# Fixed program order on four engines, with the products interleaved by hand, in a Fourier-mixing and dense-block kernel

## The chip, the cores and the metric

The kernel runs on one core of a Trainium2 chip. The metric is the time of one execution on the device in microseconds (us); lower is better. "Stop" below means time in which TensorE starts no matmul although its program has more of them. The profile calls TensorE PE, VectorE DVE, ScalarE ACT and GpSimd POOL.

## The reference, cut to what matters

```python
X = np.fft.rfft(x, axis=1)                    # x: (8, 3008, 256)
Y = X * (filt_r + 1j * filt_i)[None, :, :]
y = np.fft.irfft(Y, n=3008, axis=1)
h = y.reshape(24064, 256) @ w_in              # (256, 2048)
g = h - np.tanh(h)
return g @ w_out                              # (2048, 256)
```

## The kernel before

All arithmetic is in float32. The Fourier transforms are matmuls: `first` and `middle` (matmuls named pf, pz, pe) and `last` (pu). The two dense layers use a seven-product scheme for 2 x 2 blocks. The dense part is cut into 48 groups of tokens and 4 steps per group, 192 steps in all. In one **slot** of the loop the kernel does `up` of step U, the activation `shrink` of step U-1 and `down` of step U-2, and it weaves in the transform of the next batch unit. All transform matmuls share one PSUM bank, `up` has the three banks x, y and z, `down` the other four. X1 below is product 1 of `up`, into bank x, Y2 product 2, into bank y, and so on; p1 and p5 are ScalarE's copies of products 1 and 5 of `down`. Here is the code, shortened:

```python
    def up(U, between):
        ...
        mm(X, 1, True)
        s1 = copied("s1")             # ScalarE: PSUM -> SBUF
        mm(Y, 2, True)
        between(0)
        V.tensor_add(h[:, 0, :, 0:w], Y, s1)
        mm(X, 6, False)               # adds onto X; may start when s1 is copied
        between(1)
        u2 = copied("u2")
        mm(Z, 5, True)
        between(2)
        mm(X, 7, False)
        u3 = copied("u3")
        between(3)
        V.tensor_add(h[:, 3, :, 0:w], Z, u3)
        mm(X, 4, False)
        between(4)
        V.tensor_copy(h[:, 2, :, 0:w], X)
        mm(Z, 3, False)
        V.tensor_add(h[:, 1, :, 0:w], Z, u2)

    def shrink(U):
        for k in (2, 0):              # the two halves of h
            ACT.activation(y[k], ht[k], AF.Arctan, scale=S)
            ACT.activation(y[k], y[k], AF.Square)
            yield
            V.tensor_mul(ht[k], ht[k], y[k])
            ACT.activation(sq[k], y[k], AF.Square, bias=near_b, scale=A)
            yield
            V.scalar_tensor_tensor(out=ht[k], in0=sq[k], scalar=K, in1=ht[k], ...)
        combine(blocks, ...)          # GpSimd: four subtractions
        yield

    def down(U):                      # done: the last of a group's four steps
        mm(1, 2)
        if done: ACT.copy(p1, product(1)); V.tensor_add(...)
        yield
        mm(3, 5)
        if done: ACT.copy(p5, product(5)); V.tensor_add(...)
        yield
        mm(6, 7)
        if done: V.tensor_add(...) x2; G.tensor_add(...) x2
        yield
        mm(4)
        if done: V.tensor_add(...); store(i, o)     # two transposes on VectorE, then DMAs
        yield
```

`between(k)` takes one step of `down`, one of `shrink` and those transform steps that are due. The code only states what depends on what: a scheduler at compile time decides the order on each engine. I call the slot in which `down` finishes a group, one in four, the **closing slot**.

## Time and profile before

| | |
|---|---|
| median of 3 runs | 3037.85 us (3034.25 to 3043.77) |
| TensorE busy, of a span of 3035.6 us | 2789.7 us |
| dense part, first to last matmul | 211 to 3013 us |
| of it lost to stops and slow clock | 183 us |

From the start of each TensorE record to the start of the next I subtract the stream time of its shape (0.216 us for 256 columns). What remains is first put down to the halved clock where the trace grants one (0.50 of the full clock in its records); what then is under 0.15 us counts as "small"; the rest goes to the wait that ended it. Before: 72 us z on VectorE, 53 small, 17 slow clock, 16 x on VectorE's copy, 11 x on ScalarE's u copies, 7 transform matmuls, 6 others; with roundings 183. (The prediction took fixed ends, 210 and 3000 us, and found 180.)

How ScalarE got through a closing slot is in the timeline (start, duration, then what ran):

```profile
424.80 0.59 ACT L456 COPY u<-x 128x512 f32<-128x512 f32 x1
425.28 0.38 ACT L543 COPY p<-o 128x256 f32<-128x256 f32 x1
425.54 1.16 ACT L494 ACTIVATE sq<-y,near_b 128x1024 f32<-128x1024 f32 x1
```

The scheduler put the u copy, which TensorE needs, ahead of p5 and sq.

### The profile page before, as it was taken

The numbers are of one execution on the slowest core, as the hardware profiler recorded it, in microseconds if no ns is written. First come the engines' busy times: TensorE is split into PE (matmuls) and PEld (weight loads), VectorE is DVE, ScalarE is ACT, GpSimd is POOL, SyncE is SP. The second block draws the span as 40 slices with busy tenths as digits, with TensorE's granted clock in tenths as the row PEclk, the third lists the DMA queues.
The fourth block names the chain that finished last, engine by engine and source line by source line (L and its number), as shares of the span: only waits on it lengthen the run. The fifth ranks groups of instructions, "written<-read, shape, count | busy, mean of one in ns | idle before, by whom it ended". The sixth has DMA issues, their size and how long they took to land.

```text
span 3035.6 us, 36258 instructions
## 1 busy us (share of the span) xinstructions
PE 2789.7 (92%) x12410; PEld 2261.0 (74%) x12410; DVE 1845.8 (61%) x2382; ACT 1822.8 (60%) x2432; POOL 1602.4 (53%) x1398
## 2 busy tenths in 40 slices
PE   2369999999999999999999999999999999999996
PEld 0247766887877777887877777788888878888886
DVE  4865565665655555665665565666666666666664
ACT  1336666666666666666666666656666666666563
POOL 4653676534465566554455565645455555544543
PEclk6569999999999999999999999999999999999998
DMA  9744343222222322222322222222122212110100
GB/s 165 268 119 131 98 117 109 80 75 80 74 69 57 76 78 60 65 61 83 86 58 61 69 74 61 69 60 61 44 50 57 73 46 51 32 27 14 21 8 15
DMA packets 328867, 220.32 MB, mean 73 GB/s; under 512 B 228305, under 2 KB 282581, under 8 KB 328322
## 3 DMA queue, kind: packets, MB, share of 16 engines
q1 hardware_dynamic: 272848, 151.84, 20.1%
q10 hardware_dynamic: 53202, 50.35, 5.5%
q0 software_dynamic: 2624, 15.73, 2.0%
q8 instruction: 100, 1.64, 0.2%
q14 instruction: 93, 0.76, 0.1%
HBM read 134.41 MB, written 83.36 MB: 72 GB/s over the span
## 4 chain that ended last, share of the span: by engine, by line
PE 76%; POOL 6%; ACT 5%; DVE 5%; DMA 4%; issue 3%; ACTq 0%; SPq 0%; POOLq 0%; DVEq 0%
PE o L526 32%; PE x L450 19%; PE z L450 9%; PE y L450 5%; PE pe L338 3%; PE pu L414 3%; PE pz L357 3%; POOL t L429 2%; PE pf L283 2%; DVE h L496 1%; POOL uv L374 1%; DMA ct<-a 1%; ACT sq L494 1%; DMA w<-in_moe_w_in_dram 1%; POOL o L550 1%
## 5 line engine op out<-in xcount | busy, mean ns | idle before, releaser
L526 PE MATMUL o<-t,wd 128*128 128x256 f32 (+2 forms) x3072 | 777.4, 375 | 0.5 <-POOL t L430 0.5
L429 POOL TENSOR_TENSOR t<-h 128x512 f32<-128x512 f32 (+2 forms) x192 | 239.3, 1246 | 847.0 <-DVE h L496 754.2
L526 PEld LDWEIGHTS o<-t,wd 128*128 128x128 f32 x3072 | 577.7, 190 | 77.9 <-issue 7.8
L490 ACT ACTIVATE y<-h 128x1024 f32<-128x1024 f32 (+2 forms) x384 | 385.1, 1032 | 384.4 <-DVE h L475 384.1
L450 PE MATMUL x<-tu,wu 128*128 128x256 f32 (+2 forms) x2304 | 593.8, 378 | 6.2 <-ACT u L456 6.0
L526 PE MATMUL o<-h,wd 128*128 128x256 f32 (+2 forms) x2304 | 585.5, 376 | 3.0 <-DVE h L496 2.9
L496 DVE SCALAR_TENSOR_TENSOR h<-sq,h 128x1024 f32<-128x1024 f32 (+2 forms) x384 | 474.7, 1236 | 181.5 <-ACT sq L494 175.5
L450 PEld LDWEIGHTS x<-tu,wu 128*128 128x128 f32 x2304 | 424.2, 190 | 157.2 <-issue 84.1
L493 DVE TENSOR_TENSOR h<-h,y 128x1024 f32<-128x1024 f32 (+2 forms) x384 | 469.3, 1247 | 66.4 <-ACT y L491 64.1
L526 PEld LDWEIGHTS o<-h,wd 128*128 128x128 f32 x2304 | 436.5, 191 | 60.0 <-DVE h L496 5.3
L494 ACT ACTIVATE sq<-y,near_b 128x1024 f32<-128x1024 f32 (+2 forms) x384 | 433.8, 1130 | 76.1 <-DVE h L496 71.6
L491 ACT ACTIVATE y<-y 128x1024 f32<-128x1024 f32 (+2 forms) x384 | 386.2, 1036 | 0.9
L456 ACT COPY u<-x 128x512 f32<-128x512 f32 (+2 forms) x384 | 219.7, 572 | 217.1 <-PE x L450 206.8
L463 DVE TENSOR_TENSOR h<-y,s 128x512 f32<-128x512 f32 (+2 forms) x192 | 130.3, 679 | 268.2 <-ACT s L456 206.2
L373 POOL TENSOR_TENSOR zs<-zs,ft 128x512 f32<-128x512 f32 x112 | 143.5, 1282 | 249.1 <-ACT zs L371 234.3
L450 PE MATMUL z<-ut,wu 128*128 128x256 f32 (+2 forms) x768 | 200.5, 382 | 65.2 <-DVE h L472 64.9
L432 POOL TENSOR_TENSOR t<-t,h 128x512 f32<-128x512 f32 (+2 forms) x192 | 245.3, 1278 | 10.4
L472 DVE TENSOR_TENSOR h<-z,u 128x512 f32<-128x512 f32 (+2 forms) x192 | 129.4, 674 | 194.9 <-ACT u L456 194.9
L430 POOL TENSOR_TENSOR t<-h,t 128x512 f32<-128x512 f32 (+2 forms) x192 | 239.7, 1249 | 0.0
L431 POOL TENSOR_TENSOR t<-h 128x512 f32<-128x512 f32 (+2 forms) x192 | 239.6, 1248 | 0.0
L450 PE MATMUL x<-ut,wu 128*128 128x256 f32 (+2 forms) x768 | 218.1, 408 | 11.1 <-DVE h L475 10.7
L450 PEld LDWEIGHTS z<-ut,wu 128*128 128x128 f32 x768 | 140.5, 190 | 100.8 <-DVE h L472 82.9
(96 smaller groups left out, 3360.5 us busy)
## 6 DMA issues: line engine op xcount, KB each, us to landing
a<-ct SPq DMA_DIRECT2D x64, 384.0 KB, 3.8
ct<-e ACTq DMA_DIRECT2D x128, 192.0 KB, 2.2
ft<-filt SPq DMA_DIRECT2D x48, 512.0 KB, 4.2
out_dram<-ot SPq DMA_DIRECT2D x1408, 16.0 KB, 1.5
x_sb<-in_x_dram SPq DMA_DIRECT2D x69, 256.0 KB, 2.8
ct<-a ACTq DMA_DIRECT2D x69, 256.0 KB, 2.7
e<-ct SPq DMA_DIRECT2D x33, 512.0 KB, 4.1
filt<-filt_sb POOLq DMA_DIRECT2D x2, 4096.0 KB, 16.1
```

The source lines that it names most:

```text
L429: G.tensor_sub(t[0], b[0][1], b[0][0])
L430: G.tensor_sub(t[1], b[1][1], t[0])
L431: G.tensor_sub(t[2], b[1][1], b[0][1])
L432: G.tensor_sub(t[3], t[1], b[1][0])
L450: nc.tensor.matmul(bank[:, k], wu[:, q - 1, (2 * u + k) * 128:(2 * u + k + 1) * 128], rhs[q - 1], start=(first and k == 0), stop=True, ski ...
L456: ACT.copy(t, X)
L490: ACT.activation(y[k], ht[k], AF.Arctan, scale=S)
L491: ACT.activation(y[k], y[k], AF.Square)
L493: V.tensor_mul(ht[k], ht[k], y[k])
L494: ACT.activation(sq[k], y[k], AF.Square, bias=near_b, scale=A)
L496: V.scalar_tensor_tensor(out=ht[k], in0=sq[k], scalar=K, in1=ht[k], op0=ALU.add, op1=ALU.mult)
L526: nc.tensor.matmul(product(q), wd[:, q - 1, (2 * u + k) * 128: (2 * u + k + 1) * 128], rhs[q - 1][:, k], start=(u == 0 and k == 0 and q == ...
```

## The change

Its intent: take the order on TensorE, ScalarE, VectorE and GpSimd from the program text, and write that text so that a product and the one that depends on it are far apart. It has three parts: **(S)** strict order, **(I)** a new interleave, **(D)** the store of a group deferred to the next slot.

```diff
+            order = {nc.tensor.engine, ACT.engine, V.engine, G.engine}
+            with tc.manual_schedule(engines=order):                     # S
 ...
         mm(Y, 2, True)
-        between(0)
+        d()                                                             # I: one step of down
+        s()                                                             #    one step of shrink
         V.tensor_add(h[:, 0, :, 0:w], Y, s1)
+        t(0)                                                            #    transform steps due
         mm(X, 6, False)
-        between(1)
+        mm(Z, 5, True)
+        d()
+        s()
         u2 = copied("u2")
-        mm(Z, 5, True)
-        between(2)
+        t(1)
         mm(X, 7, False)
+        s()
         u3 = copied("u3")
-        between(3)
         V.tensor_add(h[:, 3, :, 0:w], Z, u3)
+        s()
+        d()
+        t(2)
         mm(X, 4, False)
-        between(4)
         V.tensor_copy(h[:, 2, :, 0:w], X)
+        s()
+        d()
+        t(3)
         mm(Z, 3, False)
 ...
-            store(i, o)
+            stores.append((i, o))                                       # D
 ...
+                        if k == 1 and stores:
+                            store(*stores.pop())
```

`shrink` is cut at other places too (the end of the first half goes with the start of the second). The places of `last` and of a range test at the end shift a little with the new gaps. I call the place of `t(k)` **gap k**.

More of the change, by code (lines that the diff above doesn't have):

```diff
@@ L435, with up @@
     hs, gs = {}, {}
-    def up(U, between):
+    def up(U, d, s, t):
         i, u = divmod(U, 4)
@@ L487, in shrink, with start, square, end @@
         y, sq = {}, {}
-        for k in (2, 0):
-            y[k], sq[k] = tiles("y", 2), tiles("sq", 1)
+        def start(k):
+            y[k] = tiles("y", 2)
             ACT.activation(y[k], ht[k], AF.Arctan, scale=S)
             ACT.activation(y[k], y[k], AF.Square)
-            yield
+        def square(k):
+            sq[k] = tiles("sq", 1)
             V.tensor_mul(ht[k], ht[k], y[k])
             ACT.activation(sq[k], y[k], AF.Square, bias=near_b, scale=A)
-            yield
+        def end(k):
             V.scalar_tensor_tensor(out=ht[k], in0=sq[k], scalar=K, in1=ht[k],
                                    op0=ALU.add, op1=ALU.mult)
+        start(2)
+        yield
+        square(2)
+        yield
+        end(2)
+        start(0)
+        yield
+        square(0)
+        yield
+        end(0)
         t = dn.tile([128, 4, 2, 256], F32, tag="t", bufs=2, name="t")
@@ L502, in shrink @@
         yield
-    accs = {}
+    accs, stores = {}, []
     def down(U):
@@ L754 @@
             total = 4 * len(groups)
-            for U in range(total + 2):
-                i, u = divmod(U, 4)
-                if U < total:
-                    p, c = groups[i]
-                    if c == 0 and u == 0:
-                        units = 4 * len(CHUNKS[p])
-                        steps, done = [], 0
-                        if p + 1 < len(UNITS):
-                            n_f = len(chunks_of(UNITS[p + 1], XH))
-                            n_m = 2 * NK // (3 - len(UNITS[p + 1]))
-                            steps = [(0.02 + 0.26 * k / n_f) * 4 * units for k in range(n_f)]
-                            lo, hi = 0.34 * 4 * units, 4 * units - 14
-                            steps += [lo + (hi - lo) * k / n_m for k in range(n_m)]
-                            fs, ms = first(p + 1, z1), None
-                    if u == 0 and i + 1 < len(groups) and c + 1 < len(CHUNKS[p]):
-                        e2s[i + 1] = load_e2(*groups[i + 1])
-                    if u == 2 and i + 1 < len(groups) and c + 1 == len(CHUNKS[p]):
-                        e2s[i + 1] = load_e2(*groups[i + 1])
-                    if u == 2 and i + 1 < len(groups):
-                        lasts = last(i + 1, z1)
-                sh = shrink(U - 1) if 0 <= U - 1 < total else iter(())
-                dw = down(U - 2) if 0 <= U - 2 < total else iter(())
-                def between(k):
-                    nonlocal ms, done
-                    if k < 4:
-                        next(dw, None)
-                    next(sh, None)
-                    if U >= total:
-                        return
-                    if k < 4:
@@ new lines, with d, s, t @@
+            order = {nc.tensor.engine, ACT.engine, V.engine, G.engine}
+            with tc.manual_schedule(engines=order):
+                for U in range(total + 2):
+                    i, u = divmod(U, 4)
+                    if U < total:
+                        p, c = groups[i]
+                        if c == 0 and u == 0:
+                            units = 4 * len(CHUNKS[p])
+                            steps, done = [], 0
+                            if p + 1 < len(UNITS):
+                                n_f = len(chunks_of(UNITS[p + 1], XH))
+                                n_m = 2 * NK // (3 - len(UNITS[p + 1]))
+                                steps = [(0.02 + 0.26 * k / n_f) * 4 * units for k in range(n_f)]
+                                lo, hi = 0.34 * 4 * units, 4 * units - 14
+                                steps += [lo + (hi - lo) * k / n_m for k in range(n_m)]
+                                fs, ms = first(p + 1, z1), None
+                        if u == 0 and i + 1 < len(groups) and c + 1 < len(CHUNKS[p]):
+                            e2s[i + 1] = load_e2(*groups[i + 1])
+                        if u == 2 and i + 1 < len(groups) and c + 1 == len(CHUNKS[p]):
+                            e2s[i + 1] = load_e2(*groups[i + 1])
+                        if u == 2 and i + 1 < len(groups):
+                            lasts = last(i + 1, z1)
+                    sh = shrink(U - 1) if 0 <= U - 1 < total else iter(())
+                    dw = down(U - 2) if 0 <= U - 2 < total else iter(())
+                    def d():
+                        next(dw, None)
+                    def s():
+                        next(sh, None)
+                    def t(k):
+                        nonlocal ms, done
+                        if k == 1 and stores:
+                            store(*stores.pop())
+                        if U >= total:
+                            return
@@ L794, in between @@
                             done += 1
-                    if u >= 2 and k in (1, 3) and i + 1 < len(groups):
-                        next(lasts, None)
-                    if i == len(groups) - 1 and k == 0:
-                        next(bounds, None)
-                if U < total:
-                    if i == len(groups) - 1 and u == 0:
-                        bounds = bounded(z1)
-                    up(U, between)
-                else:
-                    for k in range(5):
-                        between(k)
+                        if u >= 2 and k in (1, 2) and i + 1 < len(groups):
+                            next(lasts, None)
+                        if i == len(groups) - 1 and k in (0, 2):
+                            next(bounds, None)
+                    if U < total:
+                        if i == len(groups) - 1 and u == 0:
+                            bounds = bounded(z1)
+                        up(U, d, s, t)
+                    else:
+                        for k in range(5):
+                            s()
+                            d()
+                            t(k)
+                for w in stores:
+                    store(*w)
     within = nc.values_load(count[0:1, 0:1], min_val=0, max_val=128)
```

## The prediction

> **What bounds the kernel now.** I read the page's first part first. The profiled execution took 3035.6 us.
>
> ```profile
> PE 2789.7 (92%) x12410; PEld 2261.0 (74%) x12410; DVE 1845.8 (61%) x2382; ACT 1822.8 (60%) x2432; POOL 1602.4 (53%) x1398
> ```
>
> TensorE is the busiest by far. No other engine is near its limit, so a gain can come only from TensorE's idle time. The busy share hides how much there is, since the ends of matmuls are modelled. I therefore took pitches from the timeline: eight records of 256 columns start 1.73 us before the next instruction, 0.216 us each; two of 512 columns take 0.86 us. The groups by shape give the counts: 9632 records of 256 columns (2080 us), 672 of 192 (109), 448 of 224 (85), 748 of 128 (82), and about 255 us for the transform's matmuls inside the dense part. That is about 2610 us of pure streaming between 210 and 3000 us, a stretch of 2790. So **180 us** are lost there. It is the most that a better order can win: 3037.85 - 180 = 2858 us, 6%. The prologue (210 us) and the end are not touched; in the built program TensorE's order first differs after the first products of the dense part.
>
> Then the waits of TensorE between 228 and 2960 us (what waited, on whom: total us, times, longest):
>
> ```profile
> PE z L450 <- DVE h L472: 63.8, 39, 3.2
> PE x L450 <- DVE h L475: 10.7, 13, 2.0
> PE x L450 <- ACT u L456: 6.0, 29, 0.2
> ```
>
> One wait dominates: the last product of an "up" step waits for bank z, which VectorE has not read. The timeline of one such place (start, duration, engine, line; in brackets the idle time before it and what ended it):
>
> ```profile
> 981.40 1.03 PE L526 MATMUL o<-t,wd 128*128 128x256 f32 x4
> ...
> 983.13 1.03 PE L450 MATMUL x<-tu,wu 128*128 128x256 f32 x4
> ...
> 985.22 0.72 POOL L550 TENSOR_TENSOR o<-pu,x 128x256 f32<-128x256 f32 x1
> 985.90 0.73 POOL L551 TENSOR_TENSOR o<-p,p 128x256 f32<-128x256 f32 x1
> 985.98 0.71 DVE L569 STREAM_TRANSPOSE ot<-o 128x512 f32<-128x512 f32 x1 [4.35 <-POOL o L550]
> 986.61 0.65 DVE L472 TENSOR_TENSOR h<-z,u 128x512 f32<-128x512 f32 x1
> ...
> 987.32 1.13 PE L450 MATMUL z<-ut,wu 128*128 128x256 f32 x4 [3.16 <-DVE h L472]
> ```
>
> VectorE stands idle 4.35 us at a transpose of the finished output that waits for GpSimd, and the addition that frees z stands behind it. This happens in the "closing" slot, the one in four that finishes a group's output. I cut TensorE's records at the first product of each of the 192 up steps and subtracted the streaming time: the 48 slots with index 1 in their group lose 111 us (2.3 each), the 144 others 68 us (0.5 each). So the trace already says where the change must act.
>
> [...] in the lines above VectorE idles 4.35 us although the addition that frees z had its inputs from 982.2 us on (ScalarE's u copy, started 981.60, took 0.59). [...] here 92% busy goes with 180 us of loss in the dense part. [...] the multiplication of pz on VectorE waits for ScalarE's copy of the same bank (88.2 us, 44 times).
>
> **The change part by part.** No work is added or removed; every effect is one of order. I call 0.86 us the stream time of a product (four records). A slot of the new order is on TensorE: X1, Y2, down a (1.73), gap 0, X6, Z5, down b (1.73), gap 1, X7, down c (1.73), gap 2, X4, down d (0.86), gap 3, Z3: 12.08 us plus what the gaps hold. Latencies from the trace: end of streaming to a reader's start 0.2; PSUM copy on ScalarE 0.59 (pitch 0.47 when independent); Arctan then its own Square 1.075, next independent 0.95; sq 1.05; release of a waiting matmul 0.05.
>
> (a) The store's two transposes move to the next slot, gap 1, where the output is ready. This removes the 3 us waits above: of the 111 us nearly all.
>
> (b) Plain slot, gaps empty. ScalarE: s1 1.06, Arctan/Square to 3.7, sq to 4.7, u2 to 5.3, second pair to 7.3, u3 at 7.97 to 8.6. TensorE wants u2 at 6.90 and u3 at 9.49; bank X's last reader on VectorE ends at 11.25, wanted 12.08. No wait. Before, the last one cost 0.08 us per slot (1021.55 to 1022.52 us in the timeline: 0.97 for a product instead of 0.86). So here the interleaving works: perhaps 30 us won.
>
> (c) Closing slot. The built ScalarE order is s1, p1, Arctan, Square, p5, sq, u2. p5 must wait for down b to end (6.90): p5 at 7.1, sq 7.36, u2 8.42, done 9.05, and X7 wanted it at 6.90. Loss 2.15, less what gap 1 holds. The scheduler before had u2 ahead of p5 (u copy 424.80, p 425.28 us), which strict order gives up. Counting gap contents from the code over 47 such slots: 81 us, then X4 behind u3 14 us, and the next X1 behind VectorE's two extra additions 0.66 x some 33: 22 us. Together 117.
>
> (d) Gap 1 holds work in 110 of 192 slots. A transform matmul there ends at 7.76; ScalarE reads it (1.21 for the pair of zs copies; 0.9 for a copy and its DMA issue, which waits for the copy; 0.47 for ut), and only then starts the second Arctan pair and u3. X7 and down c give 2.59 us of cover, the chain needs 4.1, 3.75 or 3.3: losses 1.49, 1.16, 0.74, less 0.86 for each piece of work in gap 2. Over the 88 slots that do not close: 43 us, in 39 of them.
>
> (e) All transform matmuls share one PSUM bank. Where a gap holds two, the second waits in place for the first one's readers: 0.84 us, or 1.44 after a pz. I count 52 such pairs: 57 us. Where gap 1 was filled too ScalarE is late and about 1 us more falls due, some 20 times: 19.
>
> (f) z or ut work in gap 2 delays VectorE's read of X by 0.2 to 0.3: 14 us. The range test at the end is now issued in two blocks with TensorE waiting for each Abs: 8. [...]
>
> Sum (c) to (f): 117 + 43 + 57 + 19 + 14 + 18 = 268 us, against 180 before: +88, so 3126 us. I take **3120**, since a scheme that ignores every slack errs upward.
>
> **The rivals.** *Streaming rival*: the waits I list mostly vanish because the engines run ahead of my slot picture; the change then keeps (a) and (b) and ends near 2950 (90 us left). For it: the largest wait is aimed at exactly, and ScalarE is 60% busy. Against it: in (c) the wait starts from TensorE's own end of down b, so no head start of ScalarE can shorten it; and strict order leaves nothing to fill it. *Even rival*: the closing slots' loss falls to 60 and the gap pairs are cheaper because of ScalarE's earlier idle time; about 180, 3035 us. For it: before too the transform's readers stand in similar places, at 0.5 us per slot. *Worse rival*: ScalarE, VectorE and GpSimd push each other later, above all in the first quarter, where a slot holds up to six transform steps[...]; a quarter more than my sum and no shading, 3190 us. Against: GpSimd's combine (four at 1.1 to 1.25) is ready 3 us before its first use in my slot.
>
> **Range and chances.** The sum's largest term, (c), rests on a chain of measured durations; (d) and (e) rest on counts and could be off by a third each, that is 35 us, and unlisted waits by 50. Range 3035 to 3195. Faster by 2% means under 2977, a loss under 120, less than (c) alone leaves room for: 0.07. Slower means above 3099: 0.66. Within: 0.27.
>
> **What would show it.** Right: TensorE's wait on VectorE's h at the last z product (63.8 us) nearly gone; a new first wait of x on ScalarE's u copy of 100 us or more, in pieces near 2 us in closing slots (TensorE idle between down b and X7, p5 just before sq on ScalarE); pu, pe or pz waiting on ScalarE's e, zs or ut in the same gap. Wrong: the x-on-u wait stays below 40 us, or the dense part ends earlier than before; then the chain in (c) was not in the way, or ScalarE took less than I read.

Cut from this text are remarks on the hardware that no run here shows, a clause on DMA issues in the worse rival, and a term of (f): 10 us for the first products of the dense part, given without a measurement. The forecast's sum of 268 us contains that term (its last summand, 18, is 8 + 10); the terms that stand come to 258. That an instruction which waits holds up those behind it on its engine, on which (c) and (d) rest, is my reading of the trace lines above: VectorE idles 4.35 us before a transpose, with the ready addition behind it.

## More of the kernel before

The costliest groups of the page (count, then busy us and mean ns, then the engine's idle time just before them and what ended most of it):

```profile
L450 PE MATMUL x<-tu,wu 128*128 128x256 f32 (+2 forms) x2304 | 593.8, 378 | 6.2 <-ACT u L456 6.0
...
L450 PE MATMUL z<-ut,wu 128*128 128x256 f32 (+2 forms) x768 | 200.5, 382 | 65.2 <-DVE h L472 64.9
```

Of TensorE's own idle time only the group of z carries any weight.

## The result and the profile after

| | before | after |
|---|---|---|
| median, 4 runs each | 3036.05 us | 3245.11 us (3241.91 to 3250.39) |
| ratio | | 1.0685 (95%: 1.0661 to 1.0710) |
| lost in the dense part | 183 us | 397 us |

A ratio is the mean time of one kernel's fast runs over that of the other's in the same rounds, so it is not quite the ratio of the medians. The kernel became 6.9% slower. The direction was predicted; the size was not, 3245 lies above the range.

The page's first part, of the kernel after:

```profile
PE 2841.3 (88%) x12410; PEld 2309.0 (71%) x12410; DVE 1971.3 (61%) x2382; ACT 1856.8 (57%) x2432; POOL 1772.4 (55%) x1398
```

The counts of instructions are those of before. VectorE and GpSimd, however, are busy 125 and 170 us longer with the same work: some of their instructions take longer than they did (VectorE's fused one 1532 ns on average instead of 1236). The waits of TensorE in the dense part (what waited, on whom: total us, times, longest):

```profile
PE x L450 <- ACT u L456: 127.4, 98, 2.5
PE pu L414 <- DVE uv L372: 35.3, 13, 4.4
PE pe L338 <- DVE uv L372: 20.3, 15, 3.4
PE x L450 <- DVE h L480: 18.9, 31, 1.0
PE pu L414 <- ACT e L341: 14.2, 16, 1.3
```

The wait of z on VectorE is gone. In its place stand the wait of x on ScalarE's u copies (6 us before) and waits of the transform matmuls for the readers of their shared bank. A closing slot in the timeline:

```profile
730.96 0.59 PE L549 MATMUL o<-t,wd 128*128 128x256 f32 x2
731.39 1.02 PE L283 MATMUL pf<-x_sb,wf_sb 128*128 128x512 f32 x2
731.60 0.37 ACT L566 COPY p<-o 128x256 f32<-128x256 f32 x1 [0.98 <-PE o L549]
731.86 1.15 ACT L505 ACTIVATE sq<-y,near_b 128x1024 f32<-128x1024 f32 x1
...
732.91 0.57 ACT L456 COPY u<-x 128x512 f32<-128x512 f32 x1
...
733.54 1.13 PE L450 MATMUL x<-tu,wu 128*128 128x256 f32 x4 [1.13 <-ACT u L456]
```

Product X6 had been finished at 729.0 us (727.94, plus 1.03). Its copy u starts at 732.91 because p and sq stand in front, and p waits until TensorE itself has ended the second pair of `down`. TensorE starts X7 0.63 us after the copy began. In all 47 closing slots that have an `up`, ScalarE's order, transform readings left out, is s1, p1, Arctan, Square, p5, sq, u2, as the prediction has it. Next, a gap with two transform matmuls, pz and then pu:

```profile
1065.94 1.13 PE L357 MATMUL pz<-a,f 94*128 94x512 f32 x2 [2.27 <-ACT ut L416]
...
1068.44 0.69 DVE L475 TENSOR_TENSOR h<-z,u 128x512 f32<-128x512 f32 x1 [8.66 <-ACT u L456]
1069.05 1.22 DVE L504 TENSOR_TENSOR h<-h,y 128x1024 f32<-128x1024 f32 x1
...
1070.68 0.69 DVE L372 TENSOR_TENSOR uv<-pz,ft 128x512 f32<-128x512 f32 x1 [0.42 <-ACT zs L371]
...
1071.43 2.07 PE L414 MATMUL pu<-s_sb,e 128*128 128x128 f32 x8 [4.36 <-DVE uv L372]
```

This is the longest stop, and in its length it is not typical: ScalarE had stood still for 5.07 us, to 1064.94 us, before the issue of a DMA (see the last section), and all that follows on it was late. That happened twice; the 13 waits of this kind are 2.7 us on average. pu needs the bank that pz filled. VectorE's reading of pz stands behind an addition that waits for u3, and ScalarE's two readings of it behind u3 too. Then look at the duration in the last line: eight records of 128 columns take 2.07 us, where they take 1.05 at other places. The clock had been halved (granted 0.50 from 1067.1 to 1077.3 us). A table by stretches round another stop shows it (stretch, its length, TensorE's busy us, granted clock, DMA share, GB/s):

```profile
2173.50:2176.40 2.90, 0.92 (x4) 1.00 0.39 90
2176.40:2179.80 3.40, 3.40 (x11) 0.50 0.02 5
2179.80:2183.00 3.20, 3.20 (x17) 1.00 0.00 0
```

TensorE stood still from 2173.0 to 2175.5 us, and for 3.4 us afterwards it ran at half speed. Such stretches cost 65 us in the kernel after and 17 before.

### The profile page after: what moved, and what is told of

The parts are those of the page before. It is cut to its first block, busy times and chain, and to the rows that moved or that the text cites. A ratio compares the mean times of both kernels' runs of the same rounds, so it can differ in the third digit from the quotient of the medians.

```text
span 3244.4 us, 36311 instructions
## 1 busy us (share of the span) xinstructions
PE 2841.3 (88%) x12410; PEld 2309.0 (71%) x12410; DVE 1971.3 (61%) x2382; ACT 1856.8 (57%) x2432; POOL 1772.4 (55%) x1398
## 4 chain that ended last, share of the span: by engine, by line
PE 69%; ACT 13%; DVE 6%; issue 5%; DMA 3%; POOL 2%; ACTq 1%; SPq 0%; DVEq 0%; POOLq 0%
PE o L549 28%; PE x L450 18%; PE z L450 9%; PE y L450 5%; ACT y L499 3%; PE pu L414 3%; PE pe L338 3%; PE pz L357 2%; ACT u L456 2%; ACT sq L505 2%; PE pf L283 2%; DVE h L504 1%; DMA w<-in_moe_w_in_dram 1%; ACT y L500 1%; ACT zs L371 1%
## 5 line engine op out<-in xcount | busy, mean ns | idle before, releaser
L549 PE MATMUL o<-t,wd 128*128 128x256 f32 (+2 forms) x3072 | 797.5, 383 | 1.8 <-POOL t L431 1.3
L450 PE MATMUL x<-tu,wu 128*128 128x256 f32 (+2 forms) x2304 | 615.9, 391 | 132.9 <-ACT u L456 132.4
L508 DVE SCALAR_TENSOR_TENSOR h<-sq,h 128x1024 f32<-128x1024 f32 (+2 forms) x384 | 588.1, 1532 | 37.4 <-ACT sq L505 26.3
L504 DVE TENSOR_TENSOR h<-h,y 128x1024 f32<-128x1024 f32 (+2 forms) x384 | 518.2, 1350 | 111.3 <-ACT y L500 111.3
L429 POOL TENSOR_TENSOR t<-h 128x512 f32<-128x512 f32 (+2 forms) x192 | 240.1, 1250 | 602.1 <-DVE h L508 585.6
L456 ACT COPY s<-x 128x512 f32<-128x512 f32 (+2 forms) x192 | 110.8, 577 | 455.3 <-PE x L450 447.9
L432 POOL TENSOR_TENSOR t<-t,h 128x512 f32<-128x512 f32 (+2 forms) x192 | 311.3, 1621 | 0.0
L373 POOL TENSOR_TENSOR zs<-zs,ft 128x512 f32<-128x512 f32 x112 | 167.4, 1494 | 235.5 <-ACT zs L371 235.5
L431 POOL TENSOR_TENSOR t<-h 128x512 f32<-128x512 f32 (+2 forms) x192 | 295.9, 1541 | 0.0
L374 POOL TENSOR_TENSOR uv<-uv,zs 128x512 f32<-128x512 f32 x128 | 236.1, 1845 | 18.6 <-DVE uv L372 9.5
L338 PE MATMUL pe<-uv,g 112*96 112x512 f32 (+1 forms) x320 | 150.1, 573 | 72.3 <-POOL uv L374 47.2
```

The source lines that it names most:

```text
L338: nc.tensor.matmul(pe[0:RP2, i], mats[k // 4][1][:, k % 4], uv[0:IM + RP, i], start=True, stop=True)
L431: G.tensor_sub(t[2], b[1][1], b[0][1])
L432: G.tensor_sub(t[3], t[1], b[1][0])
L450: nc.tensor.matmul(bank[:, k], wu[:, q - 1, (2 * u + k) * 128:(2 * u + k + 1) * 128], rhs[q - 1], start=(first and k == 0), stop=True, ski ...
L456: ACT.copy(t, X)
L549: nc.tensor.matmul(product(q), wd[:, q - 1, (2 * u + k) * 128: (2 * u + k + 1) * 128], rhs[q - 1][:, k], start=(u == 0 and k == 0 and q == ...
```

## The experiments

Each was run with three timed rounds beside the kernel before. The results, with the loss in the dense part split as above ("x on u": waits of products of bank x for ScalarE's copies u2 and u3; "bank": waits of pf, pz, pe and pu). These losses are larger than the same waits in the lines of the profile, which count from the modelled end of the matmul before. The diffs are excerpts, against the kernel after unless another is named.

| run | time, us | ratio | lost | x on u | x on VectorE | bank | z or down on VectorE | half clock | small |
|---|---|---|---|---|---|---|---|---|---|
| before | 3036 to 3040 | | 183 | 11 | 16 | 7 | 76 | 17 | 53 |
| after | 3245 | 1.0685 | 397 | 150 | 27 | 109 | 2 | 65 | 37 |
| a1 I+D, scheduled | 2942 | 0.9676 | 87 | 1 | 30 | 14 | 5 | 13 | 22 |
| a2 S alone | 3579 | 1.1773 | 723 | 31 | 153 | 78 | 263 | 126 | 57 |
| a3 D alone | 3023 | 0.9941 | 171 | 11 | 22 | 6 | 55 | 23 | 52 |
| a4 after, u2 first | 3212 | 1.0575 | 355 | 119 | 36 | 109 | 1 | 45 | 38 |
| b1 copies first, mul late | 3165 | 1.0417 | 307 | 6 | 13 | 86 | 128 | 22 | 45 |
| b2 b1, one step per gap | 3036 | 1.0002 | 183 | 9 | 14 | 23 | 89 | 6 | 36 |
| b3 b2, scheduled | 2945 | 0.9687 | 94 | 0 | 31 | 22 | 3 | 20 | 17 |
| b4 GpSimd reads less | 3226 | 1.0617 | 378 | 149 | 26 | 101 | 2 | 60 | 36 |
| c1 one step per gap alone | 3183 | 1.0476 | 334 | 224 | 18 | 23 | 2 | 21 | 39 |
| c2 copies first alone | 3211 | 1.0577 | 358 | 6 | 119 | 137 | 3 | 47 | 37 |
| c3 b2, down reordered | 2955 | 0.9734 | 102 | 8 | 20 | 24 | 11 | 8 | 24 |
| c4 c3, scheduled | 2938 | 0.9682 | 79 | 0 | 29 | 21 | 1 | 9 | 17 |

The parts are of one profiled execution each; what is left out is under 16 us a row. All results were correct except b4's.

### First the three parts apart: a1, a2, a3

**a1**: the changed kernel without S.

```diff
-            with tc.manual_schedule(engines=order):
+            with ExitStack():
```

> The changed kernel with its hand-interleaved program order and its deferred store, but the scheduler orders the four engines again. Theory (the strict order on ScalarE and VectorE costs): TensorE's wait of x on ScalarE's u copy falls from 127 us to under 40, the kernel is at or under the one before, 2960 to 3050 us. Rival (the new product order is itself bad, as X7 stands only 2.6 us behind X6): it stays over 3150 us and the wait over 80.

Measured: 2942.3 us, 3.2% *faster* than before. TensorE's largest waits in the dense part:

```profile
PE x L450 <- DVE h L480: 28.1, 14, 3.4
PE pe L338 <- DVE uv L372: 3.5, 2, 3.3
```

x on u is 0.9 us there. The theory's cause holds, with a time below its 2960 to 3050, and the rival is out: the new order of products is good, better than the one it replaced. The trace shows what the scheduler does on ScalarE in the closing slots: u2 goes ahead of p5 in 47 of 47 and ahead of the last sq in 39, u3 ahead of the last Arctan in 47.

**a2**: the kernel before with S and nothing else (the same two lines as in the change, around the old loop).

> The kernel before with nothing changed but strict program order on the four engines. Theory (strict order costs mostly where two ScalarE works stand ahead of a copy that TensorE waits for, which the old program order does less, because u2 is wanted 2.6 us later): 3050 to 3150 us, with the wait of z on VectorE's h larger than before because the store's transposes still stand in front. Rival (strictness as such costs what was seen): 3200 us or more.

Measured: 3578.7 us, 17.7% slower than before. That is far outside the theory's 3050 to 3150 and fits the rival's number (3200 or more), though not its reason: c3 below is strict and faster than the kernel before. Its first two waits:

```profile
PE z L450 <- DVE h L472: 234.6, 139, 3.3
PE x L450 <- DVE h L475: 122.8, 161, 1.2
```

I had thought that the old program order was milder, since u2 is wanted later there. It is on that point (x on u 31 us), but X4, the copy of x and the next X1 have only the 0.86 us of Z3 between them, and Z3 itself waits for the copy u3 and an addition behind it. What makes ScalarE or VectorE late there can then stop TensorE; this is read from the code and the two waits, no run takes it apart. So the old text, read literally, is a worse program than the new one read literally (3245); it was never meant to be so read.

**a3**: the kernel before with D alone.

```diff
-            store(i, o)
+            stores.append((i, o))
 ...
                 def between(k):
                     nonlocal ms, done
+                    if k == 1 and stores:
+                        store(*stores.pop())
```

> The kernel before, scheduled, with nothing changed but the store moved to the next slot. Theory: the wait of z on VectorE's h (64 us) falls under 20, time 2965 to 3000 us. Rival (the scheduler puts the transposes back in front, or the loss moves to another wait): within 15 us of 3036.

Measured: 3023.4 us, ratio 0.9941 (0.9924 to 0.9958): a small real gain, 18 us where 40 to 70 was expected; the rival's band, within 15 us of 3036, holds it. z on VectorE goes from 72 to 51 us only. So moving the transposes mends only part of those stops. In a1, with the new interleave, the wait is down to 4.

The two-by-two table is then: old order scheduled 3039, new order scheduled 2942, old order strict 3579, new order strict 3245. I and D win 3.2%; S loses 10% on the new order and 18% on the old.

### Which part of strict order costs: a4, b4, b1, c2

**a4**: u2 ahead, u3 left where it is. TensorE's order stays the same.

```diff
         mm(X, 6, False)
+        u2 = copied("u2")
         mm(Z, 5, True)
         d()
         s()
-        u2 = copied("u2")
         t(1)
```

> The changed kernel with the u2 copy issued right behind X6, ahead of p5 and sq. Theory: the 2 us stop at X7 in the closing slots goes, but u3 still stands behind sq and the second Arctan pair, so that X4 stops for some 1.5 us there instead: gain 20 to 40 us, 3205 to 3225 us, x on u about 100 us. Rival (u2 was the whole of it): 3165 us, x on u about 50 us.

Measured: 3211.5 us, x on u still 101.6 us in the view of waits (127.4 before this edit). As the theory said, the stop moved within the closing slots: by the accounting of the table X7 falls from 79 to 2 us there and X4 rises from 16 to 63, since p5 and sq now delay the second Arctan pair instead, and u3 stands behind that.

**b4**: a wrong result, to see what the longer VectorE and GpSimd instructions are worth. In the trace of after, 212 of VectorE's 344 fused instructions of full size (L508, 128x1024) start while an instruction of GpSimd runs. They take 1.76 us on average and end 1.08 to 1.21 us after that one's end; the other 132 take 1.17 to 1.23 us. In the trace of before, 53 start so (1.46 us on average) and 291 do not (1.18 to 1.23 us). Such an overlap is called a collision here.

```diff
-        combine(blocks, [t[:, k, :, 0:w] for k in range(4)])
+        for k in range(4):
+            G.memset(t[:, k, :, 0:w], 0.5)
```

> Wrong result on purpose: the changed kernel with GpSimd's four subtractions per slot replaced by memsets of the same tiles, which read nothing. Theory (collisions of VectorE and GpSimd are real but second to ScalarE's order): VectorE's fused instruction goes from a mean of 1.55 us back to 1.25 or less, time only 20 to 70 us down, 3175 to 3225 us, x on u still over 100. Rival (the collisions are what the prediction missed): 3130 us or less.

VectorE's fused instruction in the kernel before, after and in b4, from their groups (one fence each):

```profile
L496 DVE SCALAR_TENSOR_TENSOR h<-sq,h 128x1024 f32<-128x1024 f32 (+2 forms) x384 | 474.7, 1236 | 181.5 <-ACT sq L494 175.5
```

```profile
L508 DVE SCALAR_TENSOR_TENSOR h<-sq,h 128x1024 f32<-128x1024 f32 (+2 forms) x384 | 588.1, 1532 | 37.4 <-ACT sq L505 26.3
```

```profile
L508 DVE SCALAR_TENSOR_TENSOR h<-sq,h 128x1024 f32<-128x1024 f32 (+2 forms) x384 | 516.6, 1345 | 49.1 <-ACT sq L505 37.8
```

The mean went from 1236 to 1532 ns with the change, and back to 1345 with the memsets. One collision in the trace of after: the fused instruction starts inside one of GpSimd's and takes 2.29 us, that is until the other's end at 872.46 and 1.08 us more.

```profile
871.20 1.26 POOL L432 TENSOR_TENSOR t<-t,h 128x512 f32<-128x512 f32 x1
871.25 2.29 DVE L508 SCALAR_TENSOR_TENSOR h<-sq,h 128x1024 f32<-128x1024 f32 x1
```

But the time fell by only 19 us, to 3226.4, just outside the 20 to 70 expected, and x on u stayed at 149. The memsets are also shorter than the subtractions (515 ns on average, where those take 1250 to 1621), so the 19 us are for both. The collisions are real and second-rate in this kernel. The mean did not reach 1.25; that GpSimd's other reads, which remain, are the reason is not shown.

**b1**: both copies first, and VectorE's copy of x ahead of the second half's multiplication (`s()` with it moved behind X4, the last `s()` behind Z3).

```diff
         mm(X, 6, False)
+        u2 = copied("u2")
 ...
         mm(X, 7, False)
-        s()
         u3 = copied("u3")
-        V.tensor_add(h[:, 3, :, 0:w], Z, u3)
         s()
+        V.tensor_add(h[:, 3, :, 0:w], Z, u3)
         d()
         t(2)
         mm(X, 4, False)
         V.tensor_copy(h[:, 2, :, 0:w], X)
         s()
         d()
         t(3)
         mm(Z, 3, False)
+        s()
```

> The changed kernel, strict order kept, TensorE's order untouched: ScalarE's u2 and u3 copies are issued right behind their products, VectorE's copy of x ahead of the multiplication of the second half. Theory (what stands ahead of the copies is the largest part): x on u falls from 127 us to under 35 and the slow-clock time with it, 3050 to 3110 us; the waits of pu, pe and pz for the shared bank's readers stay near 100. Rival (the longer VectorE and GpSimd instructions[...] set the pace): over 3160 us.

Measured: 3164.6 us. x on u is gone (6 us), the half clock falls from 65 to 22, but a wait that no earlier kernel had takes the first place:

```profile
PE o L549 <- DVE h L508: 104.4, 116, 1.8
```

The second half's multiplication and fused instruction now end later, and the next slot's first pair of `down` wants their result. Against the theory's 3050 to 3110 that is a miss: the size of the part removed was right, and I had not followed the delay to its next reader. The time is over the rival's 3160; whether the longer instructions or the later multiplication makes the new wait is what c2 asks.

**c2**: only the copies moved on ScalarE (b1 without the new places of the last two `s()`).

> The changed kernel, strict, with only the u2 and u3 copies moved ahead on ScalarE; VectorE's order as the changed kernel's except for what follows from it, TensorE's the same. Theory: x on u nearly goes, the wait of down a on the second half's fused instruction (104 us, which came in with the later multiplication) does not appear, but x on VectorE's copy grows to 40 to 80 us, since the multiplication in front of it now waits for the later Arctan pair: 3110 to 3160 us. Rival (VectorE's longer instructions make down a wait in any case): o on h over 60 us and 3165 us or more.

Measured: 3211.5 us, above the 3110 to 3160 expected. The new wait is where the theory put it, and larger:

```profile
PE x L450 <- DVE h L480: 100.9, 111, 1.9
PE pu L414 <- DVE uv L372: 39.0, 13, 4.5
```

The second line is hardly new, 35.3 us in the change. The rival's 3165 was passed, but its reason is out, since o does not wait on h here (1.5 us): that wait came with b1's later multiplication. So the fix of one engine's order has to be made with the others'; alone it wins 34 us where it removes a wait of 144.

### The pairs in one bank: c1, b2, c3, and the scheduled versions

**c1**: at most one transform step in a gap, six gaps per slot; copies as in the change.

```diff
         mm(Y, 2, True)
+        t(0)
         d()
 ...
         mm(Z, 5, True)
+        t(2)
         d()
 ...
-                        while done < len(steps) and steps[done] <= pos:
+                        if done < len(steps) and steps[done] <= pos:
```

(The places are renumbered 0 to 5, `last` has place 2 in the third and fourth slot of a group to itself, and the store goes to place 3.)

> The changed kernel, strict, ScalarE's order around the copies as it was, but at most one transform step in a gap and six gaps. Theory: the waits of pu, pe and pz for the shared bank (about 107 us) fall under 35 and most of the slow-clock time (65 us) goes with them, x on u stays near 130: 3080 to 3140 us. Rival (the pairs only fill time in which TensorE would wait for u anyway): 3190 us or more, x on u up by what the pairs lose.

Measured: 3182.8 us, above the theory's 3140 and below the rival's 3190. The bank's waits fall from 109 to 23 us and the half clock from 65 to 21, as expected, but x on u rises from 150 to 224:

```profile
PE x L450 <- ACT u L456: 188.7, 176, 2.3
```

That looks like the rival, in which the pairs' stops had covered ScalarE's lateness. But of the 74 us more, 51 are stops at X7 in slots that do not close, 63 of them where after has one, and in 62 a transform's reading, let in at a new place, stands ahead of u2 on ScalarE. So most of the rise comes from the new places. The half clock is telling: c1 has almost as many stops of over 1 us as after (122 and 129), but only 7 of over 2.15 us where after has 32, and a third of the slow time. In these two traces it is the long stops that go with the half clock.

**b2**: b1 with c1's gaps.

> The one before, and at most one transform step in a gap, with six gaps in a slot instead of four. Theory: the waits for the shared bank fall under 40 us, 2940 to 3010 us, so that strict order is no loss in itself. Rival (strict order costs some 100 us whatever is put right): over 3050 us.

Measured: 3036.1 us, the time of the kernel before (ratio 1.0002), not the 2940 to 3010 of the theory. The largest item left is the wait that b1 brought:

```profile
PE o L551 <- DVE h L510: 62.2, 76, 1.8
```

**c3**: b2, and the products of `down` reordered so that the first pair reads the half that is ready early (the banks of products 1 and 3 are swapped to suit, and p1's copy moves to the second pair).

```diff
-        mm(1, 2)
+        mm(2, 3)
+        yield
+        mm(1, 5)
         if done:
             ACT.copy(p1, product(1))
+            ACT.copy(p5, product(5))
             V.tensor_add(o[:, 0, 0:w], product(2), p1)
-        yield
-        mm(3, 5)
-        if done:
-            ACT.copy(p5, product(5))
             V.tensor_add(x12, product(3), p5)
         yield
```

> The strict program with copies first and one step per gap, and the first two pairs of down products ordered so that the first pair (2 and 3) needs the second half only, which is finished earlier. Theory: o on h (62 us) goes, 2960 to 2990 us. Rival (the wait moves on to the second pair, since VectorE is late by more than 1.7 us): 3010 us or more.

Measured: 2954.5 us, ratio 0.9734, a little under the theory's 2960 to 2990. TensorE's largest wait in the dense part is now

```profile
PE x L450 <- DVE h L481: 12.3, 34, 0.9
```

A strict program can thus be 2.7% faster than the kernel before; 291 us lie between it and the change, all of them order.

**b3** and **c4** are b2 and c3 with the scheduler (the one-line edit of a1).

> The same program, ordered by the scheduler. Theory (the scheduler already mends ScalarE's order, only the bank pairs are left to win): 2920 to 2945 us, at best 20 us under the scheduled interleave alone (2942). Rival (the scheduler does better only because the strict program was bad): it is slower than the strict one of this call.

> The same program ordered by the scheduler. In the scheduled interleave o waited on h for only 1 us, so theory: no gain, 2930 to 2950 us. Rival (later demand gives the scheduler freedom that it uses): under 2925 us.

Measured: 2945.1 and 2938.4 us, so no gain that stands out from a1's 2942.3 (their runs overlap). The text that strict order needs so badly is worth nothing to the scheduler. a1 and c4 beat both kernels; a1 is the change without its strict order.

## Why the prediction was right or wrong

**Right: direction and mechanism.** x on u became the first wait, with p5 and sq ahead of the copy in closing slots; the streaming rival's reason, that ScalarE runs ahead, did not hold in strict order. Step (c) and the first part of (d) put x on u at 81 + 14 + 43 = 138 us: measured 150. This is no luck of the total, since the parts fit too: X7 in closing slots 81 us predicted in 47, 79 measured in 46; X4 there 14 and 16; the other slots 43 in 39 predicted, 51 at X4 in 38 measured and 3 at X7 once. The waits of x on VectorE's copy, 22 + 14 = 36: measured 27; the first, at the X1 after a closing slot, is 10 us in 18 slots where 22 in 33 was predicted. a4 and c2 confirm by removal that it is these ScalarE orders that make the wait.

**Wrong: the sum.** Term by term, in us:

| term of the prediction | predicted | measured after |
|---|---|---|
| x on u: (c), (d) | 138 | 150 |
| x on VectorE's copy: (c), (f) | 36 | 27 |
| pairs in one bank: (e) | 57 + 19 | 109 |
| half clock; for its beginning, the term cut from (f) | 10 | 65 |
| range test and the like: (f) | 8 | 9 |
| stops under 0.15 us | 0 | 37 |
| sum | 268 | 397 |

1. **The step that failed is "against 180 before: +88".** The 268 was a list of waits worked out from zero, the 180 a total that holds everything. In the kernel before 53 us of it were small stops and 17 slow clock; my list has nothing for the first and 10 us for the second. Carried over as they were, they would have made the sum 328 and the time 3186 us, within the range. The other 69 us are terms that grew: the half clock by 48 over the kernel before, the pairs by 33 over what I had, and the rest less by 12 (the small stops fell to 37). A list of waits has to be set against the same kind of list.
2. **The 10 us for the first products of the dense part** (the term cut from (f)) had no measurement under it. I read the half clock as a matter of the beginning; in the trace of before the first two products of the dense part do take 1.71 us each at a granted clock of 0.50, instead of 0.86, which is 1.7 us in all. But in the trace of after 35 stretches of 3.4 us and more at half clock follow stops in the dense part: 65 us in place of 10, the term with the largest error. A stop of 2.15 us, the size that step (c) worked out, is of that order: of the clock steps with 1.8 to 2.2 us without streaming, 45 of 187 were followed by the half clock (last section). In c1 and b1 this part falls to 21 and 22 us with the long stops.
3. **"0.84 us, or 1.44 after a pz".** With the additional 19 this made 76 us for the pairs; measured 109. The time after a pz assumed that only ScalarE reads late. VectorE's reading stands behind an addition that waits for u3 and behind a multiplication, so the wait of pu on uv was 2.7 us on average (35.3 us in 13 times). With one step per gap (c1, b2) the pairs cost 23.
4. **"A scheme that ignores every slack errs upward"** was the reason to go from 3126 to 3120. It erred downward: what it ignored were the half clock after stops and VectorE's late readings (2 and 3). The "worse rival" named the second of these, and 3190 was still too low.

**(a) was half right.** D alone took z on VectorE from 72 to 51 us, not to nearly nothing; the rest went with the interleave. **(b)** holds: slots of full width that neither close a group nor hold anything in their gaps take 12.09 to 12.19 us from one X1 to the next in the kernel after, where 12.08 was worked out, and 3.2% are won when the rest of the order is mended (its 0.97 less 0.86 is 0.11, not 0.08; the sum does not use it). That the *streaming* figure of 2950 is within 8 us of a1 is no credit to the rival as I put it: it was reached by taking strictness away.

Collisions of VectorE and GpSimd were in no step. b4 puts the combine's reads, and what its memsets save, at 19 us. What remains open is how the 33 us of surplus in the pairs divides between them and the order of instructions: no run removed all GpSimd reads.

## What to carry to other kernels

Before fixing an engine's order by hand, write down for each copy that frees a PSUM bank which instructions stand in front of it and what they wait for; an instruction that waits for TensorE's latest work must not stand in front of one that TensorE is about to need (here p5 and sq in front of u2: 79 us at X7). Mend all engines' orders together and follow each delay to its next reader, since here every single repair moved the wait elsewhere (a4, b1, c1 and c2 won 34 to 81 us each; the copies, the later multiplication and the gaps, together with the reordered `down`, 291). And try the new program with the scheduler still on: an interleave and a fixed order are two changes, and here one was worth -3.2% and the other +10%.

## What else the traces show

- **Stops and the half clock.** In the kernel after TensorE stood still from 2173.0 to 2175.5 us, and from 2176.4 to 2179.8 the granted clock was 0.50. The traces record the clock in steps of 3.41 us: its stretches are one step long or several. I cut the dense parts of all 14 traces into these steps, left out those that were slow themselves, and added up how long TensorE streamed nothing in each. Of 11097 steps with under 1.8 us, none was followed by the half clock; of 187 with 1.8 to 2.2 us, 45 were; of 216 with more, 215. In the traces of before and after alone it is none of 1198, 4 of 21, and 40 of 40. These are counts; no run varied the length of a stop on purpose.
- **Collisions.** With VectorE 61% and GpSimd 55% busy in the kernel after, VectorE's fused instruction took 1532 ns on average instead of 1236, and the time fell by 19 us of 3245 when GpSimd's four subtractions per slot were made memsets.
- **A DMA issue in ScalarE's own order.** At 1064.94 us an issue came 5.07 us after the copy that it stores had ended, and by the profile's account the wait of the next copy was ended by the landing of another queue's load. It happened twice (5.07 and 5.08 us) in 208 issues of the dense part of the kernel after; in the 208 of the kernel before none came later than 0.68 us. Why, is open.
